# The last transform stage of a spectral filter: weights of 128 channels on each row half of TensorE in place of two times 64

## The chip, the cores and the metric

The kernel runs on one core of one Trainium2 chip. The metric is the device time of one execution in microseconds (us); the time before is the median of three runs. All arithmetic is in fp32.

## The reference

A spectral filter along the sequence, then a two-layer network with a hard-swish between its layers:

```python
# x: (8, 3008, 256); filt_r, filt_i: (1505, 256); w_in: (256, 2048); w_out: (2048, 256)
X = np.fft.rfft(x, axis=1)
Y = X * (filt_r + 1j * filt_i)[None, :, :]
y = np.fft.irfft(Y, n=3008, axis=1).reshape(24064, 256)
h = y @ w_in
g = h * np.clip(h + 3.0, 0.0, 6.0) / 6.0
out = g @ w_out
```

## The kernel before, in words

**The filter.** The sequence length is 3008 = 47 x 64. Forward and inverse transforms are each done in two stages of small matmuls with tables of sines and cosines, and between the stages the data goes through DRAM (`z_tmp`, `g_tmp`). For each of the 8 batches the stages are a (`a_unit`, `a6_unit`: 47 rows contracted), b (`b_unit`: the second stage, which gives the spectrum), the product with the filter (`f_unit`, `y_unit` on VectorE), the first inverse stage (`bi_unit`, `bi3_unit`), and the last inverse stage, which the change touches.

**The last stage.** After the first inverse stage `g_tmp` holds, for each of 64 residues, 24 frequencies with real and imaginary parts for 256 channels. `t4_load` brings up to 5 residues (a chunk) into the tile `t4`: the real parts of two mirrored residues in rows 0 to 47, the imaginary parts in rows 64 to 111. `n_five(i)` handles a chunk of five residues: for each residue `j`, each half `dh` of the 256 channels, and each of real and imaginary (`c`), it multiplies the spectrum (48 rows by channels, the weights) with the table `groups` (48 rows by 47 positions, the moving operand). The result has channels on PSUM partitions and 47 positions on columns, with one PSUM bank for each `c`. The two `c` lie on the two row halves of TensorE's array. `n_unit`, `direct` and `n_first` do the same stage for the chunks at the ends of batches, and the change does not touch them.

Behind the matmuls of a call, two ScalarE copies (`ring`, line 688) move the two banks into `xn`, a ring buffer of channels by positions. When a block of 256 position pairs is complete, `t_sums` lets GpSimd (POOL) form sums of it in the tile `xt`.

**The network.** It works on blocks of 512 tokens, held as 256 pairs, in 8 steps for the 2048 hidden channels. Each matrix product is made of seven smaller ones with sums in between. `up_1` to `up_5` make the hidden values (in the PSUM tiles `al` and `be`), `relu` on ScalarE and `hswish` on VectorE the activation, `g_sums` and `g_last` sums of it, and `down` the second layer (in the four `po` banks). All of these matmuls go through the helper `strips` (line 768 in the profile), which cuts the weights into two column halves of 64.

**The order.** It is written out by hand under `tc.manual_schedule()`. The loop over `items` goes through blocks and steps and interleaves the step's up products with the down products of the step before. The dictionary `plan` says which pieces of the filter for later batches are put into a step and at which place; `at(step, fn, ...)` fills it. A chunk's `n_five` goes either into place 0 of a step, between up and down products with two banks of the pool `psF` (tile `psn`), or into place 3, ahead of the step's up products, with the `al` and `be` banks (`ends_step=True`).

Of the kernel before, what the change touches and what calls it, by code (L numbers as in the profile page):

```python
# [27 lines left out]
NA = 47  # L28
# [3 lines left out]
P = 128  # L32
# [3 lines left out]
HALF = 64  # L36
# [21 lines left out]
ATOM = 2 * KH  # L58
# [115 lines left out]
def kernel(  # L174
# [9 lines left out]
    nc = tc.nc  # L184
# [39 lines left out]
    groups = wai[:, 0:HC * NA].rearrange("p (j n) -> p j n", n=NA)  # L224
# [7 lines left out]
    t4 = const.tile([P, 2 * NJ, D], FP32, name="t4")  # L232
# [450 lines left out]
    def ring(i, a, m_, to, out, src):  # L683
        done = 0
        while done < m_:
            r = (chunks[i][0] * HC * NA + to + done) % RING
            m = min(m_ - done, RING - r)
            nc.scalar.activation(out=out(ds(r, m)), in_=src[:, :, ds(a + done, m)], func=AXT.Copy)  # L688
            done += m

    def ready(i):
        t, n = pair(i)
        if (t + n) // PAIRS > t // PAIRS > 0:
            t_sums(t // PAIRS)


    def n_five(i, ends_step=False):
        b, js, o, n = chunks[i]
        s0 = i % 2 * NJ
        banks = [psU.tile([P, 512], FP32, name=x) for x in ("al", "be")] if ends_step else [  # L700
            psF.tile([P, 512], FP32, name="psn", tag="f") for c in range(2)]
        ps = [t[:, 0:2 * n].rearrange("p (e n) -> p e n", e=2) for t in banks]
        for q, j in enumerate(js):
            for dh in range(2):
                for g in range(2):
                    for c in range(2):
                        r = ds(c * HALF, ATOM)
                        nc.tensor.matmul(ps[c][ts(g, HALF), dh, ts(q, NA)], t4[r, s0 + q, ds(dh * P + g * HALF, HALF)],  # L708
                                         groups[r, j, :], start=True, stop=True)
        for c in range(2):  # L710
            ring(i, 0, n, o, lambda at_: xn[:, :, c, at_], ps[c])
        ready(i)
# [263 lines left out]


    EARLY = (a_unit, b_unit, bi_unit, n_unit, n_five)

    def at(step, fn, *a):  # L980
        plan.setdefault((step, 0 if fn in EARLY else 1 if fn in (w_scale, bi3_unit, a6_unit) else 2), []).append((fn, a))

    with tc.manual_schedule():
# [41 lines left out]
        ps = psU.tile([P, 512], FP32, name="al")  # L1025
# [52 lines left out]
        ps = psU.tile([P, 512], FP32, name="al")  # L1078
# [51 lines left out]
        for i in range(2, len(chunks)):  # L1130
            k = pair(i)[0] // PAIRS
            head = chunks[i][2] == 0
            same = in_block[k]
            at_, kind = same.index(i) + 1 if len(same) > 1 else 0, kinds.get(k - 1, "a")
            steps = N_FIRST[k - 1][at_] if k - 1 in N_FIRST else (FIVE_AT[kind][at_],) * 2 if len(chunks[i][1]) == NJ else N_AT[kind][at_]
            if head and len(same) == 1:
                steps = (6, 6)
            s0, s1 = ((k - 1) * NP + s for s in steps)
            five = len(chunks[i][1]) == NJ
            n_at[i] = s1  # L1140
            if head:
                stored = s0 - 3 + (k == first[1])
            at(max(stored, n_at[i - 2] + 1), t4_load, i)
            if five:
                if s1 % NP in B_AT.get(kind, ()) and len(steps) == 2 and k - 1 not in N_FIRST:
                    plan.setdefault((s1, 3), []).append((n_five, (i, True)))
                else:
                    at(s1, n_five, i)
                continue
            at(s0, n_unit, i, 0)  # L1150
            at(s1, n_unit, i, 1)
# [171 lines left out]
```

## Time and profile before

| | |
|---|---|
| median of 3 runs | 2602.28 us (2601.74 to 2604.4) |
| the profiled execution | 2602.51 us |
| its span on the core | 2600.7 us |
| granted TensorE clock | 1.0 |
| busy ACT (ScalarE) | 1298.2 us, 50% of the span |
| busy POOL (GpSimd) | 481.6 us, 19% |
| DMA traffic | 199.25 MB, 77 GB/s in the mean |
| largest groups on PE, all line 768 | `po` 1380.3 us, `al<-xt` 665.3 us, `be<-xt` 443.5 us |

How to read it: PE is TensorE's matmuls, PEld its weight loads, which run beside the matmuls, DVE is VectorE, SP is SyncE. A line such as `L708 PE MATMUL psn<-wai,t 48*64 48x47` names the source line, the engine, the tile written and the tiles read (`wai` holds the table `groups`, `t` is `t4`), the rows and columns of the weights, and the rows and columns of the moving operand. Behind the bar stand the group's busy time in us and the mean length of one record in ns, then the time that the engine stood idle before them and what ended most of it. Busy times of groups that run beside each other are unions.

### The profile page before, as it was taken

What the parts mean: (1) busy time and instruction counts of PE and PEld (TensorE: products, weight loads), DVE (VectorE), ACT (ScalarE), POOL (GpSimd) and SP (SyncE); (2) the same over time, 40 slices, a digit from 0 to 9 for tenths busy, and PEclk for the clock granted to TensorE, in tenths of its full rate; (3) what the DMA queues carried; (4) which work ended last, traced back from release to release, by engine and by line L of the source; (5) the groups of instructions that cost most, each with busy time, mean ns of one, the idle gap of its engine ahead of it and who ended that gap; (6) DMA issues with size and microseconds to landing.
All of it is one profiled execution on the core that took longest, in us unless ns stands there. A gap on an engine that the chain in (4) does not pass through costs nothing.

```text
span 2600.7 us, 87032 instructions
## 1 busy us (share of the span) xinstructions
PE 2584.9 (99%) x37890; PEld 2049.8 (79%) x37890; DVE 2026.2 (78%) x3610; ACT 1298.2 (50%) x2682; POOL 481.6 (19%) x721
## 2 busy tenths in 40 slices
PE   8999999999999999999999999999999999999999
PEld 4487777888778887788877887778877888888887
DVE  6978877887778877788777887788877888766666
ACT  4554454545544455454454544545545454455554
POOL 3252021111211112111131111311113111111110
PEclk9999999999999999999999999999999999999999
DMA  8733234213341123411233212332223421110000
GB/s 235 219 94 85 56 103 117 54 40 81 80 118 54 43 78 83 115 54 43 78 92 106 56 51 68 91 106 59 56 63 89 106 62 46 50 45 24 20 22 26
DMA packets 129843, 199.25 MB, mean 77 GB/s; under 512 B 21570, under 2 KB 97312, under 8 KB 129078
## 3 DMA queue, kind: packets, MB, share of 16 engines
q1 hardware_dynamic: 114141, 148.25, 21.1%
q0 software_dynamic: 15040, 45.21, 6.4%
q8 instruction: 297, 4.87, 0.8%
q14 instruction: 84, 0.69, 0.1%
q10 hardware_dynamic: 281, 0.24, 0.0%
HBM read 121.35 MB, written 83.98 MB: 79 GB/s over the span
## 4 chain that ended last, share of the span: by engine, by line
PE 97%; DVE 1%; DMA 1%; issue 0%; ACT 0%; SPq 0%; POOL 0%; POOLq 0%; DVEq 0%; ACTq 0%
PE po L768 45%; PE al L768 25%; PE be L768 19%; PE psf L539 1%; PE psf L480 1%; PE psn L708 1%; PE al L708 1%; PE psf L601 1%; PE be L601 1%; PE be L480 1%; DMA g_tmp<-t 0%; PE psf L768 0%; PE psf L453 0%; PE psn L768 0%; DVE g L821 0%
## 5 line engine op out<-in xcount | busy, mean ns | idle before, releaser
L768 PEld LDWEIGHTS po<-w_all,g 128*64 128x64 f32 x20808 | 1239.1, 137 | 248.5 <-issue 12.8
L768 PE MATMUL po<-w_all,g 128*64 128x128 f32 (+1 forms) x20808 | 1409.8, 274 | 1.5 <-DVE g L821 0.9
L816 ACT ACTIVATE r<-h,half_c 128x512 f32<-128x512 f32 x736 | 531.0, 721 | 322.5 <-DVE h L797 310.5
L768 PE MATMUL al<-xt,w_all 128*64 128x256 f32 x4416 | 665.3, 379 | 0.1
L821 DVE SCALAR_TENSOR_TENSOR g<-r,h 128x512 f32<-128x512 f32 x736 | 529.3, 719 | 167.0 <-ACT r L816 153.2
L768 PE MATMUL be<-xt,w_all 128*64 128x256 f32 x2944 | 443.5, 379 | 0.0
L797 DVE TENSOR_TENSOR h<-be,s 128x512 f32<-128x512 f32 x368 | 253.8, 690 | 108.8 <-PE be L768 88.5
L768 PEld LDWEIGHTS be<-xt,w_all 128*64 128x64 f32 x2944 | 212.4, 137 | 105.5
L811 ACT ACTIVATE h<-al 128x256 f32<-128x256 f32 x368 | 141.4, 384 | 286.2 <-PE al L768 285.5
L768 PEld LDWEIGHTS al<-xt,w_all 128*64 128x64 f32 x4416 | 280.2, 137 | 1.2 <-POOL w_all L357 1.0
L802 DVE TENSOR_TENSOR h<-al,s 128x256 f32<-128x256 f32 x368 | 156.2, 424 | 149.5 <-PE al L768 145.2
L829 DVE TENSOR_TENSOR g<-g 128x512 f32<-128x512 f32 x367 | 254.8, 694 | 12.6
L768 PE MATMUL al<-xn,w_all 128*64 128x256 f32 (+1 forms) x1536 | 240.5, 393 | 1.0 <-DVE g L821 0.6
L792 ACT ACTIVATE s<-al 128x256 f32<-128x256 f32 x368 | 141.5, 385 | 191.9 <-PE al L768 191.8
L768 PE MATMUL be<-xn,w_all 128*64 128x256 f32 (+1 forms) x1536 | 236.9, 388 | 0.0
L783 ACT ACTIVATE s<-be 128x256 f32<-128x256 f32 x368 | 141.4, 384 | 172.2 <-PE be L768 172.2
L763 POOL TENSOR_TENSOR xt<-xn 128x256 f32<-128x256 f32 x184 | 144.1, 825 | 358.9 <-ACT xn L688 358.9
L782 ACT ACTIVATE s<-al 128x256 f32<-128x256 f32 x368 | 141.5, 385 | 78.8 <-PE al L768 78.8
L925 POOL TENSOR_TENSOR o<-p,o 128x256 f32<-128x256 f32 x46 | 36.4, 790 | 771.6 <-DVE o L923 689.1
L828 DVE TENSOR_TENSOR g<-g 128x256 f32<-128x256 f32 x367 | 158.6, 432 | 12.6
L834 DVE TENSOR_TENSOR g<-g 128x256 f32<-128x256 f32 x367 | 157.3, 429 | 3.2
L768 PEld LDWEIGHTS be<-xn,w_all 128*64 128x64 f32 x1536 | 111.1, 137 | 61.7 <-issue 7.4
(170 smaller groups left out, 1858.3 us busy)
## 6 DMA issues: line engine op xcount, KB each, us to landing
t<-g_tmp SPq DMA_DIRECT2D x184, 120.0 KB
t<-z_tmp SPq DMA_DIRECT2D x42, 512.0 KB
g_tmp<-t POOLq DMA_DIRECT2D x68, 256.0 KB, 4.2
z_tmp<-t POOLq DMA_DIRECT2D x120, 144.0 KB, 3.4
o_tmp<-o SPq DMA_DIRECT2D x46, 256.0 KB
xs<-in_x_dram SPq DMA_DIRECT2D x60, 192.0 KB
ft<-in_filt_r_dram SPq DMA_DIRECT2D x168, 64.0 KB
ft<-in_filt_i_dram SPq DMA_DIRECT2D x168, 64.0 KB
```

The costliest lines, as they stand in the source:

```text
L763: nc.gpsimd.tensor_tensor(out=o, in0=x0, in1=x1, op=op_)
L768: nc.tensor.matmul(ps[ds(o, STRIP)], w[:, ds(o, STRIP)], x, skip_group_check=True, **kw)
L782: nc.scalar.activation(out=s[:, 0, :], in_=al, func=AXT.Copy)
L783: nc.scalar.activation(out=s5, in_=be[:, 1, :], func=AXT.Copy)
L792: nc.scalar.activation(out=s[:, 1, :], in_=al, func=AXT.Copy)
L797: nc.vector.tensor_tensor(out=st["h"][0].rearrange("p (a n) -> p a n", a=2), in0=be, in1=s, op=ALU.add)
L802: nc.vector.tensor_tensor(out=st["h"][1][:, 256:512], in0=al, in1=s5, op=ALU.add)
L816: nc.scalar.activation(out=r, in_=st["h"][i], func=AXT.Relu, bias=half_c, scale=1.0 / 6.0)
L821: nc.vector.scalar_tensor_tensor(out=st["g", k, p][:, o:o + 2, :].rearrange("p a n -> p (a n)"), in0=st["r", i], scalar=1.0, in1=st["h"][i ...
L828: v.tensor_tensor(out=g[:, G1, :], in0=g[:, G3, :], in1=g[:, G22, :], op=ALU.add)
L829: v.tensor_tensor(out=g[:, G3:G2 + 1:2, :], in0=g[:, G3:G1 + 1, :], in1=g[:, G11:G11 + 1, :].broadcast_to([P, 2, 256]), op=ALU.subtract)
L834: nc.vector.tensor_tensor(out=g[:, G4, :], in0=g[:, G12, :], in1=g[:, G2, :], op=ALU.subtract)
```

## The change

In `n_five` the inner loop over `g`, which splits 128 channels into two times 64, is dropped. Each matmul now takes 128 channels as its weights and writes all 128 partitions of its bank; the row half is still chosen by `c`. The load of the spectrum by real and imaginary rows, the tables, the banks, the copies and the order of everything else are as before.

```diff
         for q, j in enumerate(js):
             for dh in range(2):
-                for g in range(2):
-                    for c in range(2):
-                        r = ds(c * HALF, ATOM)
-                        nc.tensor.matmul(ps[c][ts(g, HALF), dh, ts(q, NA)], t4[r, s0 + q, ds(dh * P + g * HALF, HALF)],
-                                         groups[r, j, :], start=True, stop=True)
+                for c in range(2):
+                    r = ds(c * HALF, ATOM)
+                    nc.tensor.matmul(ps[c][:, dh, ts(q, NA)], t4[r, s0 + q, ts(dh, P)], groups[r, j, :], start=True, stop=True)
```

Here `HALF` is 64, `P` 128, `NA` 47, `ATOM` 48, and a chunk has `NJ` = 5 residues.

## The prediction

> **What bounds the kernel now.** I read the page first (busy time, then the chain that ended last), then the groups by line with shapes kept apart, then the chain and the timelines of TensorE and of its weight loads around a few calls of the changed helper.
>
> ```profile
> PE 2584.9 (99%) x37890; PEld 2049.8 (79%) x37890; DVE 2026.2 (78%) x3610; ACT 1298.2 (50%) x2682; POOL 481.6 (19%) x721
> ...
> PE 97%; DVE 1%; DMA 1%; issue 0%; ACT 0%; SPq 0%; POOL 0%; POOLq 0%; DVEq 0%; ACTq 0%
> ```
>
> TensorE (PE) is busy for 99% of the span and carries 97% of the chain that sets the end. A busy PE is not yet a PE at its peak, so what matters is what sets the distance between its matmuls. In the stretch from 145 to 2560 us, where nearly all calls of the changed code lie, the windows give:
>
> ```profile
> 145.00:2560.00 2415.00, 2413.54 (x36052) 1946.12 (x36050) 1888.80 (x3385) 1208.91 (x2515) 426.28 (x635) 1.00 0.26 69
> ```
>
> The first figure is the length, the second PE's busy time: PE stands still for about 1.5 us in 2415. The granted clock is 1.00. Whatever lengthens PE's work there lengthens the kernel, and whatever shortens it is a gain until another engine (DVE, at 78%) becomes late.
>
> The changed line is L708, in n_five. Its groups, beside the two other widths of weight load:
>
> ```profile
> L708 PE MATMUL psn<-wai,t 48*64 48x47 f32 x1840 | 31.8, 233 | 0.0
> L708 PE MATMUL be<-wai,t 48*64 48x47 f32 x920 | 31.6, 233 | 0.0
> L708 PEld LDWEIGHTS psn<-wai,t 48*64 48x64 f32 x1840 | 28.9, 135 | 9.3 <-issue 8.5 <-ACT r L816 0.8
> L539 PEld LDWEIGHTS psf<-t,wf 64*32 64x32 f32 x576 | 6.6, 104 | 6.9 <-issue 4.9 <-DMA ft<-in_filt_r_dram 0.4 <-DMA t<-g_tmp 0.4
> L735 PEld LDWEIGHTS po<-w_all,t 128*128 128x128 f32 x12 | 1.8, 192 | 1.2 <-issue 1.2
> ```
>
> L708 has 1840 + 920 + 920 = 3680 records (al has 920 as well). The loops of one call make 5 x 2 x 2 x 2 = 40 matmuls, and the timeline has 80 records a call, so each matmul of these fp32 operands is two records, each with a weight load of its own, and there are 3680 / 80 = 46 calls. One of them on the chain:
>
> ```profile
> 2278.82 0.86 PE be L768 x8
> 2279.68 1.31 PE psn L708 x80
> 2280.99 0.59 PE po L768 x8
> ```
>
> A call takes 1.31 us of the chain, all 46 together 60 us, 2.3% of the span. That is the most that the changed line can give. Now its rhythm, in the weight loads of another call (first column the start, second how long one took):
>
> ```profile
> 528.40 0.13 PEld L708 LDWEIGHTS al<-wai,t 48*64 48x64 f32 x1
> 528.41 0.13 PEld L708 LDWEIGHTS be<-wai,t 48*64 48x64 f32 x1
> 528.42 0.13 PEld L708 LDWEIGHTS al<-wai,t 48*64 48x64 f32 x1
> 528.42 0.13 PEld L708 LDWEIGHTS be<-wai,t 48*64 48x64 f32 x1
> 528.46 0.14 PEld L708 LDWEIGHTS al<-wai,t 48*64 48x64 f32 x1
> ...
> 528.52 0.14 PEld L708 LDWEIGHTS al<-wai,t 48*64 48x64 f32 x1
> ```
>
> Four loads, one for each quarter of the array (two row halves by c, two column halves by g), start within 20 ns. Then nothing starts for some 38 ns, and the next four follow 58 ns after the first four (528.404, 528.460, 528.518, 528.576 to the ns). So the four quarters run side by side, each with one record every 58.3 ns, and 20 such rounds make the call. The pauses between bursts say that issuing instructions is not the limit.
>
> **What sets the 58 ns.** Two candidates: the moving data (47 columns) or the weight load (64 columns). The moving data can be priced from the large matmuls:
>
> ```profile
> 2278.22 0.60 PE L768 MATMUL al<-xt,w_all 128*64 128x256 f32 x4
> 2278.65 0.60 PE L768 MATMUL be<-xn,w_all 128*64 128x256 f32 x4
> ```
>
> Four records of 256 columns on two column halves start every 0.43 us, 0.216 us for each on its half, 0.84 ns a column. 47 columns would be 39.7 ns, well under 58. The weight load is priced by the lengths above: 104, 135 and 192 ns for 32, 64 and 128 columns, so about 0.9 ns for each column on a fixed latency; 64 columns are 53 to 57 ns. That fits 58. The load is the limit of this line, and the load is what the change doubles. How fast loads of 128 columns follow each other is seen at the one place that has them with short moving data (94 columns), L735:
>
> ```profile
> 51.01 0.42 PEld L735 LDWEIGHTS po<-w_all,t 128*128 128x128 f32 x3 [0.20 <-issue]
> 51.35 0.30 PEld L735 LDWEIGHTS psn<-w_all,t 128*128 128x128 f32 x2
> ```
>
> The starts are 51.012, 51.124, 51.236 and 51.347: one every 112 ns, though 94 columns stream in 79 ns. A load of 128 columns thus paces its part of the array at 112 ns, against 58.3 for 64.
>
> **The change, part by part.** It removes 20 of the 40 matmuls of a call, which is 40 of 80 records. What stays has twice the weight columns, the same 48 rows, the same 47 moving columns and the same two PSUM banks. The two row halves (c = 0 and 1) can still run side by side; the two column halves become one load. Each row half has to take 5 x 2 x 2 = 20 records in turn before and after.
>
> The cost of a call: 20 loads in a row on each half, each longer by 112 - 58.3 = 53.6 ns. Two of the 20 differences are not a rhythm but exposed ends: at the start nothing hides the first load, and the last matmul waits for its own load. For those the same 53 to 57 ns is the difference of the load's length (192 - 135 = 57). Sum: 20 x 53.6 = 1.07 us a call, and 46 x 1.07 = 49.3 us. A call grows from 1.31 to about 2.38 us on the chain.
>
> The 112 ns comes from loads with 128 rows, the changed ones have 48. The nearest rows for the effect of rows are the 64-column loads, 135 ns with 48 rows (L708) and 137 with 128 (L768): I take it as none.
>
> What lies beside it: the matmuls' streaming (40 of the 112 ns) stays hidden under the loads. Halving the number of records saves nothing, since the bursts of 20 ns in 58 show issue slack. The two ACT copies behind each call (L688), POOL's sums for xt and the rest keep their place relative to the call's end: the same number, size and banks, and no wait is added. Behind n_five on PE stand the next down products or the L539 matmuls, and they all move back by 1.07 us, with no cover since PE is the chain. DVE, ACT and the DMAs get 1.07 us more for each call; that can only remove PE's own stalls, at most the 1.5 us of idle time in the long stretch.
>
> The change of array shape at the ends of a call costs something today: the first L708 record starts 203 ns after the start of the last 128-column record of L768 where the usual distance is 108. In 45 of the 46 calls both neighbours have another shape than n_five before and after the change, so I carry this at nothing, bounded by plus or minus 0.1 us a call (about the 95 ns seen), 4.6 us in all. In the one other (93.4 us) the L453 matmuls that follow wait 0.7 us for ACT anyway.
>
> One rule speaks for a higher price. The Trainium skill, "TensorE: Matmul & The Clock Gate", section "The mechanism", says that a weight load overlaps matmuls in flight only when their row groups differ. By that, a record would cost load and streaming one after the other on its own rows, and the sum would be nearer the third rival below. The trace disagrees for this kernel: at L735 all loads use all 128 rows, and loads of 128 columns still come every 112 ns under matmuls that stream for 79.
>
> The profiled execution took 2602.51 us (span 2600.7, so 1.8 us around it), 0.2 us from the median of the runs. 2602.5 + 49.3 = 2651.8 us, 1.9% slower.
>
> **The rivals.** First, **faster**: the load's price is not by its columns. If a load of 128 columns on half the rows took no longer than one of 64, or less, each round would fall to the streaming, 39.7 ns, and a call would save 20 x 18.6 ns = 0.37 us, 17 us in all: 2585 us. It decides once a 128-column load follows the last in under 58 ns. The Trainium skill has such a mode: the same page, section "Weight-path perf modes", has a fast weight load that comes on at 128 weights, and "TensorEngine Tiling (Array Packing)" (Restrictions) says that column tiling switches it off, so the change would be what permits it; the first page excludes fp32 from it. Against this rival stand the rows of L735: fp32, 128 columns, no column halves, and 112 ns all the same. Chance 0.05.
>
> Second, **the two row halves do not load side by side** when each load spans all columns. Then 40 loads of 112 ns stand in a row, 4.48 us against 1.17 for the 20 rounds now, 3.3 us a call, 152 us: 2754 us. For it: no row of this trace has two 128-column loads on different rows. Against: today c = 0 and c = 1 start 7 ns apart and share every round, and the 16 loads of L539 lie on both row halves as well. Chance 0.03.
>
> Third, **load and streaming in turn**: 112 + 39.7 = 152 ns a record, 20 x 93 ns = 1.87 us a call, 86 us: 2688 us. Against it L735, as said. Chance 0.02.
>
> Fourth, **nothing**: the added time falls where PE waits anyway, or the program is the same. PE's idle time in the long stretch is 1.5 us against 49 to hide, and the diff leaves no doubt that 128 columns are loaded. It would give 2602.5 us. Chance 0.02.
>
> **How the numbers follow.** My forecast has 0.88: 2651.8 us. Its own bounds: by the mean lengths 57 ns a load in place of 53.6 gives 52.4 us, and the ends of the calls add 4.6, in all 57, so 2660 us; the low end is 49.3 - 4.6 - 1.5 (stalls absorbed) = 43, so 2645. The rivals together hold 0.12, so the range of 8 in 10 is that of the forecast, and I take 2645 to 2660. About 0.2% (5 us) is what a measurement of this kernel tells from no change. Faster by more than that: the first rival, 0.05. Within: 0.02. Slower: 0.88 + 0.03 + 0.02 = 0.93.
>
> **What would show it.** In the profile after, the changed line should have 1840 records on PE (46 x 40) with loads of 48x128, a load length near 190 ns in place of 135, loads of one row half 112 ns apart with the other half's 7 ns behind, and about 2.4 us for a call on the chain. The time of L768 and of all else should be the same to a few us, and DVE's busy time too. Loads 58 ns apart or less would prove me wrong towards the first rival, loads of the two halves that alternate every 112 ns towards the second, and 150 ns towards the third; a call of 2.4 us with an end that does not move would mean that PE was not the chain.

## The result

The changed kernel takes 2650.92 us (median of 6 runs, 2649.47 to 2652.79) against 2602.88 us before: 1.0183 times as long, 95% interval 1.017 to 1.0196. The forecast was 2651.8 us. In the profiled execution the span grew from 2600.7 to 2651.0 us.

The page and the windows of the changed kernel:

```profile
PE 2635.4 (99%) x36050; PEld 2095.6 (79%) x36050; DVE 2024.4 (76%) x3610; ACT 1298.0 (49%) x2682; POOL 476.5 (18%) x721
PE 96%; DMA 1%; DVE 1%; issue 0%; ACT 0%; SPq 0%; POOL 0%; DVEq 0%; POOLq 0%; ACTq 0%
...
145.00:2610.00 2465.00, 2463.65 (x34362) 1992.84 (x34362) 1888.00 (x3389) 1210.75 (x2519) 423.75 (x639) 1.00 0.25 68
```

PE's busy time grew by 50.5 us with 1840 fewer records; DVE and ACT are as they were. PE still carries the chain and stands still for 1.4 us in the long stretch, so nothing absorbed the added time.

The changed line, now L707, in the groups with shapes apart, then one call on the chain:

```profile
L707 PE MATMUL psn<-wai,t 48*128 48x47 f32 x920 | 56.0, 286 | 0.0
L707 PEld LDWEIGHTS psn<-wai,t 48*128 48x128 f32 x920 | 53.1, 188 | 9.3 <-issue 8.1 <-ACT r L814 0.8 <-DMA o_tmp<-o 0.4
```

```profile
144.34 0.86 PE be L766 x8
145.21 2.36 PE psn L707 x40
147.57 0.47 PE po L766 x5
```

A call has 40 records in place of 80 and takes 2.36 us of the chain in place of 1.31. The length of a load is 188 ns in place of 135. The rhythm, in the timeline of weight loads of a call with the `al` and `be` banks:

```profile
431.80 0.19 PEld L707 LDWEIGHTS al<-wai,t 48*128 48x128 f32 x1
431.81 0.19 PEld L707 LDWEIGHTS be<-wai,t 48*128 48x128 f32 x1
431.91 0.19 PEld L707 LDWEIGHTS al<-wai,t 48*128 48x128 f32 x1
431.92 0.19 PEld L707 LDWEIGHTS be<-wai,t 48*128 48x128 f32 x1
432.02 0.19 PEld L707 LDWEIGHTS al<-wai,t 48*128 48x128 f32 x1
```

The two row halves (`al` is c = 0, `be` is c = 1) load 6 ns apart, and each takes its next weights 0.11 us after the last (111.7 ns over 13 rounds of another call, start to start). Before it was 58.3 ns.

46 x 1.05 us = 48.3 us of the 50.3 us. The rest is at one place, shortly after the first call, in the windows from 93 to 105 us, of the kernel before and then of the changed one (the third figure from the end is the granted clock):

```profile
93.00:105.00 12.00, 11.33 (x166) 5.83 (x162) 11.59 (x17) 6.61 (x11) 6.80 (x7) 1.00 0.47 125
```

```profile
93.00:105.00 12.00, 11.35 (x94) 6.94 (x94) 11.61 (x15) 5.05 (x9) 6.82 (x7) 0.72 0.45 137
```

The clock records of the trace have one stretch of 6.83 us at half clock from 96.1 us on, which costs up to 3.4 us. It follows the first call, behind which PE waits for ACT (0.67 us in the kernel before):

```profile
96.36 2.43 PE L453 MATMUL psf<-xs,wa 47*64 47x256 f32 x16 [0.65 <-ACT xn L688]
```

Of the six runs, this one and one other are the longest and show a mean clock of 0.998; the other four show 0.999 or 1.0. The last group of experiments asks what such a stretch is.

### The profile page after: what moved, and what is told of

Same layout as the page of the kernel before. It is cut to its first block, busy times and chain, and to the rows that moved or that the text cites. A ratio compares the mean times of both kernels' runs of the same rounds, so it can differ in the third digit from the quotient of the medians.

```text
span 2651.0 us, 83352 instructions
## 1 busy us (share of the span) xinstructions
PE 2635.4 (99%) x36050; PEld 2095.6 (79%) x36050; DVE 2024.4 (76%) x3610; ACT 1298.0 (49%) x2682; POOL 476.5 (18%) x721
## 4 chain that ended last, share of the span: by engine, by line
PE 96%; DMA 1%; DVE 1%; issue 0%; ACT 0%; SPq 0%; POOL 0%; DVEq 0%; POOLq 0%; ACTq 0%
PE po L766 43%; PE al L766 25%; PE be L766 18%; PE psn L707 2%; PE al L707 2%; PE psf L539 1%; PE psf L480 1%; PE psf L601 1%; PE be L601 1%; PE be L480 1%; DMA bits<-in_moe_w_in_dram 0%; PE psf L453 0%; PE psf L766 0%; DMA g_tmp<-t 0%; DMA w_all<-in_x_dram 0%
```

## The experiments

The theory: a round on one row half lasts as long as its slowest part, and that is the weight load, by its columns (5 ns and 0.83 ns a column, drawn through the rounds of 58.3 and 111.7 ns); the moving columns and the number of records are hidden. Rivals: the moving data adds to the load, the number of records sets the pace, or the parts of the array hinder each other.

**Weights of 96 columns.** Changed kernel with

```diff
-  nc.tensor.matmul(ps[c][:, dh, ts(q, NA)], t4[r, s0 + q, ts(dh, P)], groups[r, j, :], ...)
+  nc.tensor.matmul(ps[c][0:96, dh, ts(q, NA)], t4[r, s0 + q, ds(dh * P, 96)], groups[r, j, :], ...)
```

> As the changed kernel, but with weights of 96 channels in place of 128 (32 of each 128 channels are left out of the matmuls and the copies). Theory of the columns (a row half takes its next weights after 5 ns and 0.83 ns a column): a round of 85 ns, midway between 58.3 and 111.7, so 46 x 20 x 26.7 ns = 24.6 us less than the changed kernel, about 2626 us. Rival, a fixed price of the wide shape (any weights over 64 columns cost the same round): 2651 us.

Measured: 2625.11 us, 1.0085 times before (1.0068 to 1.0102), where 64 columns are 1 and 128 columns 1.0183. Its loads and a call on its chain:

```profile
L707 PEld LDWEIGHTS psn<-wai,t 48*96 48x96 f32 x920 | 40.9, 162 | 9.3 <-issue 8.5 <-ACT r L814 0.8
```

```profile
2300.49 1.83 PE psn L707 x40
```

The call (1.83 us) stands midway between 1.31 and 2.36, and the load (162 ns) between 135 and 188. The price goes by columns; the wide shape has no fixed price.

**88 moving columns in place of 47**, on the kernel before and on the changed one (shown for the latter; `banks[c]` is the whole bank, and the loop over `dh` is outside so that the next residue overwrites the surplus):

```diff
-  nc.tensor.matmul(ps[c][:, dh, ts(q, NA)], t4[r, s0 + q, ts(dh, P)], groups[r, j, :], ...)
+  nc.tensor.matmul(banks[c][:, ds(dh * n + q * NA, 88)], t4[r, s0 + q, ts(dh, P)], wai[r, ds(j * NA, 88)], ...)
```

> As the kernel before (two times 64 columns), but with 88 moving columns in place of 47; the 41 surplus results are overwritten by the next residue. Theory of the columns: the load of 64 columns (58 ns) is overtaken by streaming, 88 x 0.84 + 2 = 76 ns a round, so 46 x 20 x 17.7 ns = 16 us slower, 2619 us. If load and streaming add up, 41 x 0.84 = 34 ns a round, 32 us, 2634 us. If issue sets the 58 ns, nothing: 2602 us.

> As the changed kernel (128 columns), but with 88 moving columns in place of 47. Theory of the columns: 76 ns of streaming stay hidden under a load of 112 ns, no change from the changed kernel, 2651 us (within 3). If load and streaming add up: 34 ns a round more, 2682 us.

Measured: on the kernel before 2620.16 us, 1.0066 (1.0051 to 1.0081), that is 17 us slower; on the changed kernel 2651.0 us, 1.0185 (1.017 to 1.02), the same as the changed kernel with 47. A call on the chain of each:

```profile
2320.76 1.68 PE psn L708 x80
```

```profile
2322.65 2.40 PE psn L707 x40
```

Nearly doubling the moving data lengthens a call by 0.37 us where loads take 58 ns, and by 0.04 us where they take 112. The rounds of the kernel before grow from 58.3 to 76 ns, and those of the changed kernel stay at 112. Load and streaming lie over each other, and the longer one counts. Addition would have given 32 us in both.

**One column half, one place.** First the kernel before with `for g in range(1)`, then 128 columns only where the banks are `al` and `be` (`for g in range(1 if ends_step else 2)`, with weights of 128 or 64).

> As the kernel before, but with only the first of the two column halves (the other 64 of each 128 channels are left out of the matmuls and the copies): half of the records. Theory of the columns: the column halves load side by side, the round stays 58 ns, 2602 us (within 3). If the 58 ns come from the number of records, a round falls to the streaming of 42 ns: 15 us faster, 2587 us.

> 128 columns only in the 23 calls that use the al and be banks, two times 64 in the other 23. Each call costs 1.05 us on the chain whatever its neighbours: 23 x 1.05 = 24.2 us slower than before, 2627 us. If the place mattered (a call ahead of the L539 matmuls against one ahead of the down products), it would be further from the middle.

Measured: one column half 2600.46 us, 0.999 (0.9981 to 1.0); half of the calls 2625.76 us, 1.0086 (1.0071 to 1.0101). A call with one column half, and the two groups of the mixed kernel:

```profile
2303.33 1.30 PE psn L708 x40
```

```profile
L708 PE MATMUL al<-wai,t 48*128 48x47 f32 x460 | 55.8, 286 | 0.0
L708 PE MATMUL psn<-wai,t 48*64 48x47 f32 x1840 | 31.8, 233 | 0.0
```

Half the records, the same 1.30 us: the number of records is not what paces the kernel before, and its second column half costs next to nothing. That is what the change gives away: one load of 128 columns (112 ns) takes about as long as two loads of 64 one after the other, and before the two ran side by side. The price of a call is the same at both places within the noise: half of the calls cost 22.4 us, all of them 48.0, and in the changed kernel a call takes 2.36 or 2.37 us of the chain at either place.

**Four times 32.** The kernel before with `for g in range(4)` and 32 channels each.

> The other way: four times 32 channels, eight tiles of the array, 80 matmuls a call. Theory of the columns: the load of 32 columns falls to about 32 ns and no longer limits; streaming is 42 ns, and eight records of 6.6 ns issue (the distance inside a burst of L539) 53 ns, which is then the bound: 46 x 20 x 5.5 ns = 5 us faster than before, 2597 us. If issue does not bind, 15 us faster, 2587 us. If more matmuls cost by their number, about twice a call: 2655 us.

Measured: 2679.13 us, 1.0295 (1.028 to 1.031), 76 us slower. A miss, in sign too. The shortest calls, first record to last, take 1.44 us in place of 1.15: 72 ns a round, 9 ns a record. In such a call the first 32 records start 6.6 ns apart; then, after a pause of 0.1 us, two start every 16.7 ns, round after round. Such an even spacing, with no pause between rounds, speaks for issue as the bound, and a tighter one than the 6.6 ns of the short L539 group suggested; no run tried it apart from the narrower weights. Other calls stop for up to 3.7 us in their middle. The waits name almost nothing but issue for it (time in which the profile shows nothing that the engine waited for):

```profile
PEld psn L708 <- issue: 22.7, 32, 2.6
PEld be L708 <- issue: 16.7, 7, 3.6
PE psn L708 <- issue: 12.9, 10, 2.5
PE be L708 <- issue: 10.2, 4, 3.5
```

All idle time ahead of L708 put down to issue, PE and PEld together, is 78 us here (12 us in the kernel before), with 160 records a call in place of 80. Why TensorE's records come late was not tried. Eleven stretches at half clock add to it, each 3.41 us and each behind 1.6 to 2.9 us of idle PE; ten of them lie in or behind a call, one ahead of the first. Of the 76 us, 46 x 0.29 = 13 us are the longer rounds, 38 us what the calls last beyond 1.44 us each, and up to 19 us the clock; 6 us stay open. So the kernel before has the width that is best of the three: 64 columns are bound by the load, 128 by a longer load, and 32, as it seems, by issue.

**One row half, and the clock.** The second rival of the prediction was that the row halves hinder each other. The changed kernel with `for c in range(1)`, the result copied twice:

> As the changed kernel, but with only the real rows (c = 0); its result is copied in place of the imaginary part too. Half of the records, all on one row half. Theory of the columns: the row halves load side by side, 20 loads in a row stay, a round of 112 ns, 2651 us (within 3). If the two halves hinder each other's loads, the time falls, by up to 49 us to 2602.

Measured: 2682.61 us (2675.49 to 2683.86), 1.0298 (1.0283 to 1.0314): with half of the matmuls left out, 31 us slower than the changed kernel. No theory had that. The call itself is as the theory of the columns has it, 2.36 us on the chain:

```profile
252.54 2.36 PE psn L707 x20
```

So the row halves do not hinder each other. The time is lost behind the call. The windows around it:

```profile
250.00:256.00 6.00, 6.00 (x64) 4.91 (x62) 5.42 (x10) 3.26 (x7) 2.29 (x4) 0.96 0.50 117
256.00:259.00 3.00, 3.00 (x26) 2.49 (x24) 0.69 (x1) 1.10 (x2) 2.82 (x4) 0.52 0.24 82
259.00:262.00 3.00, 3.00 (x48) 2.59 (x46) 2.59 (x5) 1.11 (x3) 2.90 (x4) 1.00 0.00 0
```

PE is busy throughout, but from 256 to 259 us its granted clock is 0.52, and it starts 26 records where the next 3 us have 48. The trace's clock records hold 16 such stretches up to the last block, each 3.41 us at half clock, and each begins 0.3 to 1.4 us after the last record of a call of n_five. 16 x 3.41 / 2 = 27.3 us. With these, and without the changed kernel's own stretch (3.4 us), its span of 2651.0 becomes 2674.9 us, and the span here was 2673.6. This execution is the shortest of the four; the other three show a clock of 0.986 in place of its 0.99.

Why 16 of 46 calls? The stretches at full clock between the 16 last 12 to 96 times 3.413 us, whole multiples all, so in this trace the clock changes on a grid of that step. Laid on the grid, 14 of the 46 calls lie wholly within one step, and a stretch follows each of the 14. Of the 32 calls that a border of the grid cuts, only two are followed by one; they begin 15 and 144 ns before a step. PE is never idle in the steps ahead of the 16 stretches.

Two runs asked whether the little use of the array in the call is the cause. Both have one row half; the first streams 88 columns in place of 47, the second has two times 64 columns, as the kernel before.

> As the run with one row half (128 columns, c = 0 alone), but with 88 moving columns in place of 47; the surplus results are overwritten. The rounds stay load-bound at 112 ns, so a call takes as long as before, but the array streams 76 of 112 ns in place of 42. Theory of the clock (the granted clock halves for 3.4 us behind a call in which the array did too little): fewer or no such dips, and the time falls towards 2651 us although there is more work. Rival (the dips and the extra 31 us come from something else, as the length of the call or the order of its records): 2682 us as without the added columns, or more.

> As the kernel before (two times 64 columns, a round of 58 ns), but with the real rows alone; their result is copied in place of the imaginary part too. Half of the records. Theory of the columns: 20 loads in a row remain, 2602 us (within 3). Theory of the clock: the array is as little used as in the run with one row half and 128 columns, but for 1.2 us a call in place of 2.2, so fewer dips, between 2602 and 2620 us.

Measured: with 88 moving columns 2654.28 us, 1.0196 (1.0181 to 1.0211), 28 us faster than with 47, though the array does more; with two times 64 columns 2602.42 us, 0.9999 (0.9989 to 1.0008). A long window of the run with 47 moving columns, of the one with 88, and of the one with two times 64 columns (the clock is the third figure from the end), then a call of the last:

```profile
105.00:2590.00 2485.00, 2483.94 (x33230) 1994.02 (x33230) 1880.50 (x3380) 1206.78 (x2507) 435.36 (x673) 0.99 0.25 69
```

```profile
105.00:2590.00 2485.00, 2483.51 (x33540) 1998.64 (x33538) 1902.54 (x3404) 1219.79 (x2537) 445.95 (x680) 1.00 0.25 69
```

```profile
105.00:2590.00 2485.00, 2483.41 (x35152) 1994.76 (x35150) 1940.20 (x3468) 1245.47 (x2591) 451.12 (x680) 1.00 0.25 70
```

```profile
2277.81 1.30 PE psn L708 x40
```

With 88 moving columns none of the 16 stretches is left, although 11 calls lie wholly within one step of the grid. The one stretch that this run has (3.41 us at 98.7 us) is behind the first call, where PE waits 0.53 us for ACT. The run with two times 64 columns has none before its last microseconds. The changed kernel streams as little a round as the run with 47 columns, but on both row halves, and 14 of its later calls lie within one step without a stretch; its only one follows the first call, whose step holds 0.41 us of idle PE as well. So calls of this length, where they lie within one step, cost clock when the array streams for about 42 of 112 ns on one row half alone, and not when it streams more or on both halves: idle PE is not needed for it.

The run with two times 64 columns does not show that short calls are spared. Its expectation took the array for as little used as with 128 columns, but 42 ns of streaming in a round of 58 is as large a share as 76 in 112. So the length of the call was not tried apart from the streaming. Nor was the order of the loops, which the run with 88 columns changes too, or where the threshold lies.

## Why the prediction was right

**What bounds it.** That PE's time goes to the end one to one held: 48.3 us in the calls, and 1.5 and 1.4 us of idle time in the long stretch before and after.

**The load as the limit.** The step that carried the forecast was to take the pace of 128-column loads from L735, the one place in the profile with such loads and short moving data. It read 112 ns there; the changed line has 111.7. The 128 rows there against 48 here made no difference. That row alone left one thing open: 112 ns could also have been 79 ns of streaming and a shorter load in turn. It is ruled out by the same 112 ns with 47 and with 88 moving columns. The run with 96 columns and the two with 88 moving columns show the mechanism, not only the sum.

**The size.** 2.38 us forecast for a call, 2.36 measured. The array's change of shape, carried at nothing within 0.1 us, is nothing at the start: the first record comes 203 or 309 ns after its predecessor, in both kernels. At the end, the next matmul starts 215 ns after the call's last in place of 161; that is the exposed load already in the sum of 20. The sum took 18 rounds and two exposed ends; the trace has 19 rounds (1.15 us became 2.15) and the one at the end, which comes to the same. That the forecast lies within 1 us of the median is in part luck: the six runs spread over 3.3 us, and the sum holds nothing for the clock.

**The rule weighed.** "TensorE: Matmul & The Clock Gate" of the Trainium skill, section "The mechanism", has loads overlap matmuls only on other row groups. With a single row half in use the rounds are 112 ns with 47 moving columns and the same with 88. Streaming is about 42 and 76 ns of them (an estimate from the rounds of 76 ns for 88 columns and the 216 ns for 256), so here a load does overlap a matmul on its own rows.

**The rivals.** Faster by a quick load of 128 columns: no, 188 ns. Row halves in turn: no, 6 ns apart, and one alone takes as long as two. Load and streaming in turn: no, rounds of 112 and not 152 ns. Nothing: no, 48 us.

**What it missed.** It took the clock for fixed. The profiled execution of the changed kernel has one stretch at half clock that the kernel before has not, up to 3.4 us, and with one row half left out there are 16, 27 us. No rival named that.

## What to carry to other kernels

When matmuls on small tiles of the array stream few columns, price a round as the longest of three: the weight load by its columns, the moving columns, and the records issued. Cutting weights into column halves lets their loads run side by side, so fewer and wider matmuls can be slower although they do the same work; look for a row of the trace with the wide load and short moving data, and read its start-to-start time. Cutting further did not help here (four times 32 columns were 76 us slower), and a stretch of thinly used array can cost clock afterwards, so look at the granted clock beside the busy time.

## What was not expected of the hardware

- The granted clock halves for 3.41 us although PE was never idle: 16 times in the run with one row half (2.36 us calls, 47 columns streamed in each round of 112 ns, on half of the rows), none of these with 88 moving columns, and none in the kernel before until its last microseconds. The stretches lie on a grid of 3.413 us, and the calls that lie within one step of it have them.
- Work added to a kernel made it faster: 2654.28 us with 88 moving columns against 2682.61 us with 47, on one row half.
- With eight tiles in use, the first 32 records of a call start 6.6 ns apart and the rest two in 16.7 ns, and a call of 160 records often stops, for up to 3.7 us, with no wait that the profile shows.
